# One feature map moved four and six steps sooner, its DMA transpose seven steps sooner and one matrix product one step later, in a fused attention and mixer kernel

## The chip, the cores and the metric

The kernel runs on one core of one Trainium2 chip. The metric is the device time in microseconds of one execution; smaller is better. All executions told of here ran at a granted TensorE clock of 0.99 to 1.00.

## The reference

Eight batches go through a linear attention and then through an MLP mixer. `phi` is the feature map elu(x) + 1.

```python
q_p, k_p = phi(q), phi(k)
kv = einsum('bhsd,bhse->bhde', k_p, v)
num = einsum('bhsd,bhde->bhse', q_p, kv)
den = einsum('bhsd,bhd->bhs', q_p, k_p.sum(axis=2))[..., None] + 1e-06
x = (num / den)                                   # to [batch, seq, 512]
h = maximum(x.transpose(0, 2, 1) @ w_tok1, 0) @ w_tok2
u = x + h.transpose(0, 2, 1)                      # token mixing
out = u + maximum(u @ w_ch1, 0) @ w_ch2           # channel mixing
```

## The kernel before

The program is one hand-ordered stream. The channel mixing of the batch pair that is ready is the "big" work of TensorE: `mm3` is the product with `w_ch1` (tile c_ps, line L480), `mm3_tail` the same for the rows left over (L494), `mm4` the product with `w_ch2` (h_ps, L506). A list `fill` names the step of this big work after which each small piece of the next batches' attention and token mixing is placed. The part that matters is the stage in which batches 0 and 1 finish, batch 2 is mixed and batch 3 is prepared.

```python
def phi(nm, n, c):                       # half c of batch n: exp on ScalarE, add and min on VectorE
    phi_exp(nm, n, 2 * c, 2); phi_add(nm, n, 2 * c, 2); phi_end(nm, n, 2 * c, 2)

def qtr_dma(n):                          # two DMA transposes, issued on SyncE: qp -> qT
    for a in range(2):
        nc.sync.dma_start_transpose(out=qT[n % 2][...], in_=qp[half[a]]...)   # ... cut

def utr_dma(n, rs):                      # u -> uT, half of the rows each
    nc.sync.dma_start_transpose(out=uT[b][...], in_=u[b][...])                # ... cut

def mm1(n): ...    # first mixing product, tile a_ps (L246); ScalarE writes relu to ar (L249)
def mm2(n, rs): ...# second mixing product, tile h_ps (L259); VectorE adds x and writes u (L271)
def nd_mm(n, c, rs): ...   # numerator and denominator, tile nd_ps (L208); qT is the weights

def mm4_end(p, t):                       # VectorE writes o_sb; every second tile two stores of 256 KB
    ...
    put = nc.sync if last else nc.gpsimd     # here: GpSimd
    (nc.scalar if last and e else put).dma_start(out=outv[...], in_=live["o"][half[e], 0:m])   # ... cut

def run(bigs, fill):
    for i, big in enumerate(bigs):
        big()
        for s, fn in fill:
            if s == i: fn()

# the stage in question: 3 + 9 steps of mm3, 3 of mm3_tail, 15 of mm4 (tiles 4 to 8)
at1 = {"kv": 8, "nd00": 10, ..., "nd21": 15,
       "mm1": 17, "mm2a": 18, "mm2b": 19, "mm2t": 21, "uta": 18, "utb": 19}
fill += [(at1[nm], fn) for nm, fn in steps(2)]
fill += [(s, lambda g=g: phi("q", 3, g)) for g, s in ((0, 19), (1, 22))]
fill += [(23, lambda: qtr_dma(3)), (23, lambda: load_all(4, "qkv"))]
fill += [(s, lambda g=g: prep_k(3, g)) for g, s in ((0, 24), (1, 26))]
run(big, sorted(fill, key=lambda e: e[0]))
# the next stage starts with mm3(2), which reads uT of batch 2; after its step 3 comes nd of batch 3, which reads qT
```

## Time and profile before

| | kernel before |
|---|---|
| time, median of 3 runs | 264.59 us (264.04 to 264.92) |
| span in the profile | 263.6 us |
| TensorE busy | 252.5 us, 96% |
| its one full stop after the start-up | 2.6 us, at 89.7 to 92.3 us |

A row of the timeline or of the chain is read as start in us, length in us, engine, line, operation, tiles (output, then inputs), count; what stands in square brackets is how long the engine had been idle and what ended that. Rows of the same operation are merged, so a row's length includes pauses between its instructions. The important rows are shown by the prediction below. One more view puts the stop into proportion: the busy time of each engine in two stretches of the kernel before (start and end, length, then busy time and instructions of TensorE, its weight loads, VectorE, ScalarE, GpSimd, then clock, DMA share and GB/s):

```profile
68.00:85.00 17.00, 16.91 (x83) 7.64 (x81) 11.60 (x20) 7.99 (x9) 1.53 (x3) 1.00 0.45 64
85.00:93.00 8.00, 5.42 (x97) 2.72 (x96) 1.70 (x5) 3.14 (x6) 1.93 (x4) 1.00 1.09 231
```

TensorE is full in the first stretch and lacks 2.58 us in the second, while the packet records fill the time of the 16 DMA engines (a share of 1.09; it is over 1 because records overlap, up to 28 at once in this stretch).

### The profile page before, as it was taken

The page shows a single profiled execution, that of the slowest core. Times are in us where ns is not written, and L with a number is a line of the kernel's source. Part 1 is how long each engine was busy: PE and PEld are TensorE (multiplying, and loading weights), DVE is VectorE, ACT ScalarE, POOL GpSimd, SP SyncE. Part 2 cuts the span into 40 slices and gives each one's busy share as a digit, 9 for nine tenths or more (in the row PEclk, how much of TensorE's full clock was granted, in tenths as well). Part 3 has the DMA queues.
Part 4 walks back from the last instruction along what each step waited for, and adds up shares of the span by engine and source line. Part 5 has one row for each costly group of instructions (what it writes and reads, how often), then busy time and mean ns, then how long its engine had stood idle before and what let it go on. Part 6 is the DMA issues. An engine that isn't in the chain of part 4 may idle for free.

```text
span 263.6 us, 5060 instructions
## 1 busy us (share of the span) xinstructions
PE 252.5 (96%) x2070; PEld 131.5 (50%) x2070; DVE 146.3 (56%) x283; ACT 130.8 (50%) x205; POOL 35.4 (13%) x58
## 2 busy tenths in 40 slices
PE   7789999999999699999999999999999999999994
PEld 3574465646644254445554554455564554444642
DVE  5865769866659185848564285838564272520122
ACT  5756763387292448425871368425870363027300
POOL 9660210110003100030001300030001300000000
PEclk9999999999999999999999999999999999999999
DMA  7999999999129992699998980761085500940043
GB/s 252 248 204 271 382 205 397 233 254 409 41 40 139 223 405 104 137 230 360 410 335 205 344 320 1 160 150 42 0 111 140 123 0 0 152 109 0 2 99 100
DMA packets 50087, 48.34 MB, mean 183 GB/s; under 512 B 30288, under 2 KB 35536, under 8 KB 50064
## 3 DMA queue, kind: packets, MB, share of 16 engines
q1 hardware_dynamic: 41904, 35.53, 46.0%
q0 software_dynamic: 7440, 11.44, 21.3%
q10 hardware_dynamic: 720, 1.05, 1.2%
q8 instruction: 16, 0.26, 0.4%
q14 instruction: 7, 0.06, 0.1%
HBM read 35.85 MB, written 9.44 MB: 172 GB/s over the span
## 4 chain that ended last, share of the span: by engine, by line
PE 80%; DMA 11%; ACT 3%; POOL 3%; issue 0%; SPq 0%; DVE 0%; ACTq 0%; POOLq 0%
PE h_ps L506 33%; PE c_ps L480 26%; PE a_ps L246 6%; PE c_ps L494 4%; DMA k_raw<-in_k_dram 4%; PE h_ps L259 4%; DMA wc<-in_moe_w_ch_dram 4%; DMA qT<-qp 3%; PE nd_ps L208 3%; PE kv_ps L167 2%; ACT e L124 1%; PE h_ps L543 1%; POOL qT L587 1%; ACT cr L487 1%; POOL cr L116 1%; PE h_ps L280 1%
## 5 line engine op out<-in xcount | busy, mean ns | idle before, releaser
L480 PE MATMUL c_ps<-uT,wc 128*128 128x512 bf16 x384 | 91.5, 379 | 0.0
L487 ACT ACTIVATE cr<-c_ps 128x512 bf16<-128x512 f32 x91 | 53.2, 599 | 77.1 <-PE c_ps L480 77.1
L506 PE MATMUL h_ps<-wc,cr 128*128 128x512 bf16 x372 | 85.1, 379 | 0.2
L506 PEld LDWEIGHTS <-cr 128*128 128x128 bf16 x372 | 35.7, 98 | 41.9 <-issue 1.6
L480 PEld LDWEIGHTS <-wc 128*128 128x128 bf16 x384 | 35.8, 98 | 36.7 <-issue 1.3
L528 POOL DMA_DIRECT2D out_dram<-o_sb x24 | 14.5, 606 | 153.2 <-DVE o_sb L523 152.9
L523 DVE TENSOR_TENSOR o_sb<-h_ps,u 128x512 f32<-128x512 f32 x31 | 21.2, 689 | 23.6 <-PE h_ps L506 23.4
L220 DVE TENSOR_TENSOR x<-nd_ps,den 128x512 bf16<-128x512 f32 (+1 forms) x42 | 25.3, 602 | 1.4
L124 ACT ACTIVATE e<-q_raw 128x1152 bf16<-128x1152 f32 x16 | 18.5, 1163 | 6.3 <-DMA q_raw<-in_q_dram 6.1
L271 DVE TENSOR_TENSOR u<-h_ps,x 128x1024 bf16<-128x1024 f32 x12 | 14.7, 1222 | 11.2 <-PE h_ps L259 11.2
L124 ACT ACTIVATE e<-k_raw 128x1152 bf16<-128x1152 f32 x16 | 18.7, 1168 | 4.2 <-DMA k_raw<-in_k_dram 4.2
L138 DVE TENSOR_TENSOR qp<-e,y 128x1152 bf16<-128x1152 bf16 x16 | 12.1, 759 | 13.6 <-ACT e L124 13.1
L217 DVE TENSOR_SCALAR den<-nd_ps 128x8 f32<-128x8 f32 (+1 forms) x42 | 6.8, 163 | 22.1 <-PE nd_ps L208 21.4
L208 PE MATMUL nd_ps<-kvbd,qT 128*128 128x130 bf16 x140 | 15.3, 223 | 2.6 <-DMA qT<-qp 2.6
L208 PEld LDWEIGHTS <-qT 128*128 128x128 bf16 x140 | 11.3, 98 | 12.0 <-DMA qT<-qp 2.9
L138 DVE TENSOR_TENSOR kp<-e,y 128x1152 bf16<-128x1152 bf16 x16 | 12.1, 756 | 8.0 <-ACT e L124 7.4
L246 PE MATMUL a_ps<-x,w 128*128 128x512 bf16 x56 | 14.4, 379 | 0.0
L149 ACT CAST vs<-v_raw 128x1152 bf16<-128x1152 f32 x12 | 13.9, 1159 | 0.0
L130 DVE TENSOR_SCALAR y<-k_raw 128x1152 bf16<-128x1152 f32 x16 | 12.0, 753 | 2.8 <-DMA k_raw<-in_k_dram 2.7
L533 DVE TENSOR_TENSOR o_sb<-h_ps,ut 128x512 f32<-128x512 f32 x4 | 2.8, 689 | 18.7 <-PE h_ps L506 18.7
L249 ACT ACTIVATE ar<-a_ps 128x512 bf16<-128x512 f32 x14 | 7.6, 594 | 10.9 <-PE a_ps L246 10.9
L259 PE MATMUL h_ps<-ar,w2p 128*128 128x512 bf16 x48 | 12.5, 379 | 0.1
(102 smaller groups left out, 207.9 us busy)
## 6 DMA issues: line engine op xcount, KB each, us to landing
k_raw<-in_k_dram SPq DMA_DIRECT2D x16, 576.0 KB, 9.0
q_raw<-in_q_dram SPq DMA_DIRECT2D x16, 576.0 KB, 7.7
v_raw<-in_v_dram SPq DMA_DIRECT2D x14, 576.0 KB, 11.0
out_dram<-o_sb POOLq DMA_DIRECT2D x24, 256.0 KB, 4.4
wc<-in_moe_w_ch_dram POOLq DMA_DIRECT2D x8, 384.0 KB, 10.3
out_dram<-o_sb SPq DMA_DIRECT2D x9, 128.0 KB, 2.3
out_dram<-o_sb ACTq DMA_DIRECT2D x7, 128.0 KB, 2.6
out_dram<-o_sb POOLq DMA_DIRECT2D x6, 128.0 KB, 5.9
```

The lines of the kernel that those rows point to most:

```text
L124: nc.scalar.activation(out=e, in_=f, func=AF.Exp)
L138: nc.vector.tensor_tensor(out=dst.transpose([0, 2, 1, 3]), in0=e.rearrange("p (i t d) -> p i t d", i=nj, t=T), in1=y.rearrange("p (i t d) ...
L208: nc.tensor.matmul(out=o[:, a], lhsT=qT[b][:, t0:t0 + 128], rhs=kvbd[b][:, c, a], start=True, stop=True)
L220: nc.vector.tensor_tensor(out=x[b][:, rs[0]:rs[0] + m, HG * D * g:HG * D * (g + 1)].rearrange("p r (h d) -> p r h d", h=HG), in0=v_[:, :, ...
L246: nc.tensor.matmul(out=ps[:, mt], lhsT=w1t[:, b, ms] if r == R else w1[:, r, ms], rhs=x[b][:, r, :], start=(r == 0), stop=(r == R))
L259: nc.tensor.matmul(out=ps[:, i], lhsT=w2v(kt, r, b), rhs=ar[b][:, kt, :], start=(kt == 0), stop=(kt == NT - 1 and not add))
L271: nc.vector.tensor_tensor(out=u[b][:, rs[0]:rs[0] + m], in0=ps[:, 0:m], in1=x[b][:, rs[0]:rs[0] + m], op=ALU.add)
L480: nc.tensor.matmul(out=ps, lhsT=wc1[:, kj, 128 * mc:128 * mc + 128], rhs=uT[b][:, :, kj], start=(kj == 0), stop=(kj == NDM - 1))
L487: nc.scalar.activation(out=cr[b][:, mc, :], in_=ps, func=AF.Relu)
L506: nc.tensor.matmul(out=ps, lhsT=crt[:, kc, :] if t == 8 else cr[b][:, kc, 128 * r:128 * r + 128], rhs=wc2[:, kc, :], start=(kc == 0), stop ...
L523: nc.vector.tensor_tensor(out=o, in0=ps, in1=u[b][:, r, :], op=ALU.add)
L528: (nc.scalar if last and e else put).dma_start(out=outv[2 * p + b, :, 2 * r0 + e:2 * r0 + e + 2 * m - 1:2], in_=live["o"][half[e], 0:m])
```

## The change

The intent: batch 3's q features exist earlier, so that their transpose is done long before its reader; and the second mixing product of batch 2 no longer follows so close behind the first that it waits for ScalarE's relu. The whole diff:

```diff
     at1 = {"kv": 8, "nd00": 10, "nd01": 11, "nd10": 12, "nd11": 13, "nd20": 14, "nd21": 15,
-           "mm1": 17, "mm2a": 18, "mm2b": 19, "mm2t": 21, "uta": 18, "utb": 19}
+           "mm1": 17, "mm2a": 19, "mm2b": 20, "mm2t": 21, "uta": 19, "utb": 20}
     fill = [(s, lambda g=g: phi("k", 2, g)) for g, s in ((0, 0), (1, 2))]
     fill += [(4, lambda: vcast(2, 0)), (5, lambda: vcast(2, 1, nc.vector.tensor_copy))]
     fill += [(at1[nm], fn) for nm, fn in steps(2)]
-    fill += [(s, lambda g=g: phi("q", 3, g)) for g, s in ((0, 19), (1, 22))]
-    fill += [(23, lambda: qtr_dma(3)), (23, lambda: load_all(4, "qkv"))]
+    fill += [(s, lambda g=g: phi("q", 3, g)) for g, s in ((0, 15), (1, 16))]
+    fill += [(16, lambda: qtr_dma(3)), (23, lambda: load_all(4, "qkv"))]
```

## The prediction

> **What bounds the kernel now.** I read the first part of the page, then the chain of waits in order of time, then who waited for whom, then the timeline around the one stretch that does not fit.
>
> ```profile
> PE 252.5 (96%) x2070; PEld 131.5 (50%) x2070; DVE 146.3 (56%) x283; ACT 130.8 (50%) x205; POOL 35.4 (13%) x58
> ```
>
> TensorE is busy 96% of the 263.6 us, everything else about half. So only TensorE's own idle time can be won, and other engines matter where they make it wait. The chain of the middle of the run is matmuls end to end except here:
>
> ```profile
> 70.86 2.17 PE a_ps L246 x10
> ...
> 73.56 0.60 ACT ar L249
> 74.20 0.81 PE h_ps L259 x3
> ...
> 76.73 6.87 PE h_ps L506 x32
> 83.60 8.62 DMA qT<-qp
> 92.27 0.35 PE nd_ps L208 x3
> ```
>
> The columns are start, length, what. Two things hang on something other than TensorE: at 73.56 to 74.20 ScalarE's relu eviction (ar) between the first mixing product of batch 2 (a_ps) and its second (h_ps L259), and at 83.60 to 92.27 a DMA transpose that brings batch 3's q features (qp) into the layout qT that the numerator/denominator product (nd_ps) loads as weights. The view of waits for TensorE alone, from 52 us to the end, has one line, so after the start-up this is the only full stop there is:
>
> ```profile
> PE nd_ps L208 <- DMA qT<-qp: 2.6, 1, 2.6
> ```
>
> The timeline shows how it came about (start, length, engine, line, how many):
>
> ```profile
> 73.06 1.08 ACT L249 ACTIVATE ar<-a_ps 128x512 bf16<-128x512 f32 x2 [4.39 <-PE a_ps L246]
> 73.72 1.28 PE L259 MATMUL h_ps<-ar,w2p 128*128 128x512 bf16 x4
> 76.29 2.96 SPq L464 DMA_TRANSPOSE uT<-u  x2
> 80.41 1.20 POOL L528 DMA_DIRECT2D out_dram<-o_sb  x2 [24.81 <-DVE o_sb L523]
> 80.88 0.76 DVE L138 TENSOR_TENSOR qp<-e,y 128x1152 bf16<-128x1152 bf16 x1
> 81.70 4.42 SPq L197 DMA_TRANSPOSE qT<-qp  x2
> 84.66 1.20 POOL L528 DMA_DIRECT2D out_dram<-o_sb  x2 [3.06 <-DVE o_sb L523]
> 85.20 1.89 PE L480 MATMUL c_ps<-uT,wc 128*128 128x512 bf16 x8
> 92.27 0.35 PE L208 MATMUL nd_ps<-kvbd,qT 128*128 128x130 bf16 x3 [2.58 <-DMA qT<-qp]
> ```
>
> The transposes are issued at 81.70, the moment the last qp is written (80.88 + 0.76), and then land slowly:
>
> ```profile
> DMA to landing us min/median/max: 5.5/7.1/8.6
> ```
>
> That line is for the two transposes of this stretch; over all twelve the same view gives 3.6/3.8/8.6. Two pairs of output stores (issued at 80.41 and 84.66, 256 KB each store) share the 16 DMA engines with them. Counting packets by size in the trace: from 82 to 84 us, 81 store packets of 4096 B and only 13 transpose packets of 256 B started; where transposes run alone (107 to 113 us) some 630 to 780 of them start per us. The 0.25 us at 73.72 is the other loss: four matmuls took 1.28 where the same four took 1.03 at 75.70, because the second half of ar ends only at 74.14.
>
> [...] the loads issued on SyncE from 86.22 on start to move (2304 B packets) only at 90 us, when the transpose before them is through. [...] Here about 700 packets of 256 B per us is some 180 GB/s[...], while 2304 B loads run at about 400 GB/s (94 to 96 us). The measured rate is used below. [...] Here the matmuls of the stages stand end to end at their steady 0.86 us per four, so the 96% does mean that the engine's stream is full.
>
> **The change, part by part.** No instruction is added or removed; comparing the order of instructions, TensorE takes four L506 matmuls ahead of the two groups of h_ps L259, VectorE and ScalarE move the q feature map ahead, SyncE issues qT before uT.
>
> *Feature map of q(3) to steps 15 and 16, transposes to 16.* ScalarE stands idle 4.39 us before 73.06, so the two exponentials (2.22 us for both) fit in 68.7 to 70.9 at no cost; their input landed at 61.2. VectorE's last x of batch 2 ends at 70.01; two adds and two mins (0.75 and 0.76 each, 3.1 us together) then run to about 73.1. It was idle 3.45 us before 75.04, so the next needed output (u) is not delayed, only the store staging of output tile 4, whose PSUM bank is not wanted until 82.6. The transposes then issue at about 73.2 and 74.6, with no other DMA in flight (last load landed at 68.1). At the 3.8 us median they land at 77.0 and 78.4, ten us ahead of the need at 89.7. **Gain: 2.58 us**, all of it on the path, because TensorE has no other wait later to absorb it.
>
> *Second mixing product one step later.* Between a_ps and h_ps now stand eight L506 matmuls (1.73 us) instead of four (0.86): a_ps ends at 73.02, so h_ps starts at 74.75, after ar is done at 74.14. **Gain: 0.25 us.** It delays u: the halves end on TensorE at 75.6 and 77.3 instead of 75.0 and 76.7, so u is written by about 76.9 and 78.7, and the two uT transposes issue at about 76.9 and 78.8 instead of 76.29 and 78.02.
>
> *What this collides with.* Before, the second uT landed 4.33 us after issue, at 82.35; its reader (c_ps at 85.20) had 2.85 us to spare. With 0.25 us won, the reader now comes at 84.95. A landing as fast as before would be at about 83.1: 1.8 us to spare. But the first pair of stores, which in the kernel before was held back to 80.41 by the q feature map on VectorE, now leaves at about 77.6 and 78.2: in front of the second uT, and the second pair comes at about 83.3. That is the position in which the first qT stood before (stores 1.29 and 0.70 us ahead of it): it needed 5.49 us. 78.8 + 5.5 = 84.3, still 0.65 us in time. By packets: about 128 store packets at 0.4 us each over 16 engines are 3.2 us, 78.7 to 81.9, in which transposes hardly move; some 1,600 of uT's 2,048 packets are then left, 2.4 us at 670 per us, to 84.3, and 0.7 us to the semaphore: 85.0. So the reader waits between nothing and about 1 us, and some 2.5 us if the second pair of stores also gets in front. I put the mean at **0.4 us** (half the chance on none, three in ten on up to 1 us, two in ten on more; the last are partly bounded because the stores must first be written).
>
> *Sum.* 264.59 - 2.58 - 0.25 + 0.4 = 262.2; as no wait is the likeliest single case (261.8), I say 262.1.
>
> **Rivals.**
> 1. *uT takes qT's place as the late transfer.* For it: the working above, under 1 us of slack by either estimate. [...] At worst, a landing 8.6 us after issue (as the second qT did) is 87.4, a wait of 2.45 us, which leaves 264.59 - 2.83 + 2.45 = 264.2: no visible gain.
> 2. *The transfer was hidden anyway, or another input is late at the same place.* nd_ps also needs kvbd, but ScalarE wrote that by 88.62, and one nd_ps matmul ran at 89.47, before the stop. I give this little weight. It would leave at least 263.5.
> 3. *VectorE or ScalarE becomes the bound around 70 us.* If the feature map got in front of ar or of batch 2's last x, mm1 would wait up to 2 us: 264. The order on each engine shows it behind x and in a 4.39 us hole of ScalarE, so I nearly rule it out.
> 4. *Later stages give it back.* From 92 us on, all loads, transposes and stores shift with the matmuls; uT has 4.7 us to spare at 115.37 (landed 110.62) and 7.2 at 147.24 (landed 140.07). Batch 4's loads even leave earlier, at about 80 instead of 86.22. I see nothing to give back.
>
> **Range and chances.** Full gain is 261.8; runs of one kernel spread by about 0.4 us to each side, so the low end is 261.3. A wait for uT of some 1.5 us plus spread gives 263.7 at the high end. Two per cent is 5.3 us, twice all the idle time there is to win, and the worst rival ends at parity: the chance of within 2% is 0.98, with 0.01 to each side.
>
> **What would show it.** Right: the wait of nd_ps for qT is gone from TensorE's waits, the qT transposes issue at about 73 and land within 4 us, h_ps L259 takes 1.03 per four without a pause after ar, SyncE's uT issues near 77 and 79. For rival 1 look for a new wait of c_ps L480 or its weights for uT at about 85 us; its length is what is lost. Wrong for me would be: a uT wait over 1.5 us, a pause before a_ps at 70.9, or a new stop past 95 us.

## The result, and the profile after

| | before | after |
|---|---|---|
| time, median of 6 runs | 264.61 us (263.84 to 264.92) | 262.45 us (262.01 to 262.63) |
| ratio, with 95% interval | | 0.9922 (0.9906 to 0.9938) |
| span in the profile | 263.6 us | 260.4 us |
| TensorE waits of the view from 52 us on | one, 2.6 us | none |

A ratio is the mean time of one kernel's fast runs over the mean of the other's of the same rounds, so it is not quite the ratio of the medians. Executions over 1.5% slower than the fastest of the same kernel are left out of the means. The change saves 2.2 us of the median: real, but within 2%.

The chain of waits after, at the places that answer to those of before (start, length, what):

```profile
72.89 1.73 PE h_ps L506 x8
74.62 0.86 PE h_ps L259 x4
...
84.98 1.73 PE c_ps L480 x8
86.70 0.71 PE kv_ps L167 x70
87.41 1.83 PE c_ps L480 x8
89.25 0.23 PE nd_ps L208 x4
```

The step over ScalarE and the DMA transpose are out of the chain: every row is TensorE, each starting where the row before it ends. The timeline of the kernel after:

```profile
72.93 1.09 ACT L249 ACTIVATE ar<-a_ps 128x512 bf16<-128x512 f32 x2 [2.28 <-PE a_ps L246]
72.99 2.75 SPq L197 DMA_TRANSPOSE qT<-qp  x2
74.45 1.03 PE L259 MATMUL h_ps<-ar,w2p 128*128 128x512 bf16 x4
76.77 3.75 SPq L464 DMA_TRANSPOSE uT<-u  x2
77.64 1.20 POOL L528 DMA_DIRECT2D out_dram<-o_sb  x2 [22.18 <-DVE o_sb L523]
84.81 1.89 PE L480 MATMUL c_ps<-uT,wc 128*128 128x512 bf16 x8
89.08 0.40 PE L208 MATMUL nd_ps<-kvbd,qT 128*128 128x130 bf16 x4
```

The transposes of q are issued at 73.0, not 81.7; h_ps takes 1.03 us for its four, not 1.28; and nd_ps runs its four at 89.08 without a stop. The stores leave at 77.6, between the two transposes of u. Time from issue to landing of the two q transposes, and then of the two u transposes, in the kernel after (least, median, most):

```profile
DMA to landing us min/median/max: 3.4/3.6/3.7
DMA to landing us min/median/max: 3.1/4.4/5.7
```

So q is no longer slowed, and u is: its second half, issued at 78.50, landed at 84.22, 0.6 us before its reader at 84.81. The two stretches of the table above, in the kernel after:

```profile
68.00:85.00 17.00, 16.89 (x80) 7.76 (x80) 12.26 (x21) 7.93 (x9) 2.40 (x4) 1.00 0.58 131
85.00:93.00 8.00, 8.00 (x118) 4.37 (x117) 3.95 (x11) 4.75 (x9) 1.07 (x2) 1.00 1.01 356
```

The second stretch is full. (A few matmul records are missing from the trace after; counts of matmuls are not compared.)

**An accounting that does not close yet.** The two profiles differ by 3.1 us of span, the medians by 2.16 us. From the first mixing product (70.86 before, 70.73 after) to the end of the first nd_ps group (92.62 and 89.48) the profiles differ by 21.76 - 18.75 = 3.01 us. Of that, 0.26 lies ahead of c_ps (the pause after ar), and 2.75 between c_ps and the end of the group: the stop of 2.58 and 0.17 for starting the matmuls again (0.22 + 0.35 against 0.40 us for the group). So the profile of before showed a gain larger than the timed runs had. The experiments had to explain that too.

### The profile page after: what moved, and what is told of

Its sections match the earlier page's. It is cut to its first block, busy times and chain, and to the rows that moved or that the text cites. A ratio compares the mean times of both kernels' runs of the same rounds, so it can differ in the third digit from the quotient of the medians.

```text
span 260.4 us, 5043 instructions
## 1 busy us (share of the span) xinstructions
PE 251.7 (97%) x2052; PEld 131.7 (51%) x2070; DVE 146.3 (56%) x283; ACT 130.8 (50%) x205; POOL 35.4 (14%) x58
## 4 chain that ended last, share of the span: by engine, by line
PE 88%; POOL 4%; DMA 3%; ACT 3%; DVE 1%; issue 1%; POOLq 0%
PE h_ps L506 33%; PE c_ps L480 32%; PE a_ps L246 5%; PE c_ps L494 4%; PE h_ps L259 4%; PE nd_ps L208 3%; DMA w<-in_moe_w_tok_dram 3%; PE kv_ps L167 2%; POOL w2p L451 1%; PE h_ps L543 1%; ACT e L124 1%; POOL qT L587 1%; POOL cr L116 1%; PE h_ps L280 1%; ACT cr L487 1%
## 5 line engine op out<-in xcount | busy, mean ns | idle before, releaser
L130 DVE TENSOR_SCALAR y<-q_raw 128x1152 bf16<-128x1152 f32 x16 | 12.2, 765 | 0.0
```

The lines of the kernel that those rows point to most:

```text
L130: nc.vector.tensor_scalar(out=y, in0=f, scalar1=1.0, scalar2=1.0, op0=ALU.add, op1=ALU.max)
```

## The experiments

**Theories.** (A) The stop exists because store packets get in front of the q transposes on the DMA engines. It is then a race, whose length differs from run to run. (B) The stop has a fixed length of 2.6 us and the transposes were simply issued too late; the 0.7 us between the sum of the prediction (2.83 us) and the 2.16 us measured are then a new wait for uT, in timed runs but not in the profile. And: do the two parts of the change add up, as the prediction has it?

Eleven runs were made. Eight are in the table; b1 to b3, the kernel before profiled again, follow it.

| run | what | median us (range), 6 runs | before in the same rounds | ratio (95%) |
|---|---|---|---|---|
| c0_after | the change, again | 262.25 (262.09 to 262.62) | 263.79 (262.39 to 264.75) | 0.9946 (0.9919 to 0.9973) |
| e1_q_only | only the q part | 262.45 (262.26 to 263.06) | as above | 0.9952 (0.9927 to 0.9978) |
| e6_after_stores_held | the change, first stores held | 262.2 (261.91 to 262.5) | as above | 0.994 (0.9915 to 0.9965) |
| e4_before_stores_held | before, all four stores held | 262.21 (261.98 to 262.92) | as above | 0.9943 (0.9918 to 0.9969) |
| e2_mm2_only | only the mixing product | 262.5 (262.29 to 262.76) | 264.44 (263.72 to 265.59) | 0.9926 (0.9908 to 0.9944) |
| e3_map_only | the change, transposes late | 263.52 (263.33 to 264.3) | as above | 0.9969 (0.9947 to 0.999) |
| e5_mm2_later | the change, product yet later | 262.23 (261.82 to 262.5) | as above | 0.9915 (0.9896 to 0.9933) |
| e7_pair2_held | before, second stores held | 262.59 (262.22 to 262.89) | 264.29 (262.59 to 266.45), 10 fast runs | 0.9939 (0.99 to 0.9979) |

All gave correct results. One thing shows at once: the 11 runs of the kernel before spread over 2.4 and 1.9 us in the first two lots (6 runs over 1.1 us in the first comparison), the 6 runs of every version without the stop over 0.5 to 0.9 us. (In the third lot the kernel before has, beside the slow run, one of 266.45 us at a clock of 0.994, counted as fast; without these two its spread is 2.0 us. That run also flatters the ratio of e7.)

### The kernel before, profiled three more times

No edit.

> The kernel before again, for another profile. Theory (the stop for qT is a race between transpose and store packets, and so differs from run to run, which is why the timed runs of this kernel spread from 262.4 to 264.9 us): a wait between 0 and 2.6 us, and the run's time is about 262.4 us plus this wait. Rival (the stop is always 2.6 us, and the spread is from elsewhere): a wait of 2.5 to 2.7 us whatever the run's time.

> The kernel before once more, for its profile. Theory (the stop is a race and differs): wait plus 262.4 us gives this run's time within 0.5 us; the wait is anything from 0 to 2.6 us. Rival: 2.5 to 2.7 us again.

> The kernel before once more, for its profile. Theory and rival as for the one just before: the wait differs between 0 and 2.6 us and accounts for the run's time over 262.4 us, or it is 2.5 to 2.7 us whatever the time.

The line of TensorE's waits from 52 us on, in the runs b1, b2 and b3, in this order:

```profile
PE nd_ps L208 <- DMA qT<-qp: 1.9, 1, 1.9
```

```profile
PE nd_ps L208 <- DMA qT<-qp: 1.2, 1, 1.2
```

```profile
PE nd_ps L208 <- DMA qT<-qp: 1.2, 1, 1.2
```

| profile of before | wait us | time of that run us | time less wait |
|---|---|---|---|
| the first | 2.58 | 265.34 | 262.76 |
| b1 | 1.86 | 264.31 | 262.45 |
| b2 | 1.19 | 263.81 | 262.62 |
| b3 | 1.18 | 263.94 | 262.76 |

(b1 to b3 are single runs, of unknown state; their clock was 0.998 to 1.0.) The wait is not fixed, and what is left after taking it away is the same within 0.3 us. The profile that the prediction was made from had the longest stop of the four, and its run, 265.34 us, was slower than all three timed runs that the prediction quotes. That closes the accounting: the timed runs' stop is on the mean shorter than 2.6 us. The last column has a mean of 262.65 us, so the median of 264.61 us holds, by estimate, a stop of 1.96 us; the 0.20 us that are left of the 2.16 us fit the shorter pause after ar. The fastest runs of the kernel before, 262.39 and 262.59 us, leave no room for more than a few tenths of a stop; none of those was profiled, so that they had none is an inference.

### Stores held, in the kernel before and in the kernel after

The edit keeps the stores of some output tiles back until a given transpose has landed (a dependency of the store on that transfer). It is shortened here:

```diff
-                    (nc.scalar if last and e else put).dma_start(out=outv[...], in_=live["o"][half[e], 0:m])
+                    # as a closure that is called later, with a dependency on the gate
+                    after(put.dma_start(out=outv[...], in_=o[half[e], 0:m]), gate)
+    # e4: fill += [(23, lambda: release(5, "qT_dma")), (27, lambda: release(7, "qT_dma"))]
+    # e7: fill += [(27, lambda: release(7, "qT_dma"))]
+    # e6: fill += [(20, lambda: release(5, "uT_dma"))]
```

e4 holds both pairs in the kernel before, where nothing else is moved.

> The kernel before with nothing moved, except that the stores of output tiles 4 to 7 of the first pair of batches wait until the second qT transpose has landed. Theory (the transposes were late because store packets held them up): qT lands within 4 us of issue, near 85.6 and 87, before the need at 89.5; the stop of 2.6 us is gone; the pause of 0.25 us after ar stays; time 0.25 us over the changed kernel, about 262.7 us. Rival (issue at 81.7 is simply too late, or something else slows the transposes): qT still lands after 89.5, time over 263.7 us.

Issue to landing of its two q transposes, and what its stores waited for:

```profile
DMA to landing us min/median/max: 3.5/3.7/3.8
```

```profile
87.17 2.39 POOL L535 DMA_DIRECT2D out_dram<-o_sb  x4 [31.84 <-DMA qT<-qp]
```

The transposes were issued at 81.4 and 82.8, as late as before, and landed at 85.0 and 86.6, well ahead of nd_ps at 89.2. There is no TensorE wait, and the time is that of the changed kernel. The stores alone made the transposes late (3.5 and 3.8 us from issue to landing here, 5.2 to 8.6 us in the four profiles of the kernel before); the late issue did not. The pause after ar is still there (1.28 us for the four matmuls of h_ps), yet the median is not 0.25 us over c0 as expected; differences of 0.2 us are within what these medians can tell.

e7 holds only the second pair.

> The kernel before with only the second pair of stores (output tiles 6 and 7) held until the second qT transpose has landed; the first pair goes as before. In the kernel before, 63 packets of one of these stores ran between the two qT transposes. Theory[...]: qT a is late as before, landing 5.5 us after issue near 87; qT b follows it at once and lands near 88.5 to 89.0, just before the need at 89.2 to 89.5; no wait or under 0.3 us; 262.3 to 262.8 us. Rival (the first pair alone makes qT too late): qT b lands after 90.5, a wait over 1 us, over 263.4 us.

Issue to landing of its two q transposes:

```profile
DMA to landing us min/median/max: 4.9/5.3/5.8
```

The first, behind the first pair of stores, took 5.8 us, as in the kernel before (5.2 to 5.8 in its four profiles). The second took 4.9 us instead of 7.2 to 8.6, landed at 88.5, and nd_ps did not stop. Packets started per microsecond show what went with it (store packets are 4096 B, transpose packets 256 B; counted from the traces):

```text
            kernel before              e7: second pair held
from us   stores  transposes         stores  transposes
 82          46        0                48        0
 83          35       13                39       19
 84          25      132                23      207
 85           5      479                 2      537
 86          37      536                 0      890
 87          26      214                 0      650
 88           1      540                 0        1
 89          15      354                 0        0
```

In the kernel before, most of one 256 KB store (63 packets at 86 and 87 us) runs between the two transposes, and the pair's second store runs among the last 86 packets of the second transpose (from 89.75 us on). Holding the pair takes away both, and the stop with them; which of the two stores costs more was not tested. The picture also differs from profile to profile: at 86 and 87 us the four profiles of the kernel before start 63, 22, 32 and 36 store packets, at 88 and 89 us 16, 105, 89 and 99. In all four the second transpose lands within 0.4 us of the pair's second store (92.22 and 92.06 us in the first).

The columns also show uneven counts, though less than the first rows suggest. Where no store is about (after, c0, e1, e4, e5, e6), the first packet of the first q transpose starts 1.18 or 1.19 us after its issue. With that delay after the issue at 81.70, no transpose packet was to be expected here before 82.88 us; from 82.88 to 84 us the kernel before started 43 store packets and 13 transpose packets.

e6 holds the first pair in the changed kernel, to see whether its timed runs hide a wait for uT.

> The changed kernel with the first pair of stores of this stage held until the second uT transpose has landed. Both: uT b lands within 4.3 us of its issue instead of 5.7. Theory: no change of time, within 0.15 us of the changed kernel, as uT was in time. Rival (hidden uT wait in the timed runs): 0.3 to 0.7 us faster than the changed kernel.

Issue to landing of its two u transposes:

```profile
DMA to landing us min/median/max: 3.1/3.6/4.1
```

uT's second half landed 4.1 us after its issue instead of 5.7 (at 82.3), and the median went from 262.25 to 262.2 us. Nearly two microseconds of slack more bought nothing, so the changed kernel does not wait for uT to a degree that these medians can show. Theory B's hidden wait, expected to be worth 0.3 to 0.7 us here, is not seen.

### Each part alone

e1 has only the q part:

```diff
-           "mm1": 17, "mm2a": 19, "mm2b": 20, ..., "uta": 19, "utb": 20}      # of the kernel after
+           "mm1": 17, "mm2a": 18, "mm2b": 19, ..., "uta": 18, "utb": 19}
```

> The q feature map and its transposes early, the second mixing product at its old steps. Theory (the stop for qT is all gone, uT is in time in the changed kernel's timed runs too): loses the 0.25 us pause after ar again, so 0.25 us over the changed kernel, about 262.7 us; uT b lands near 82.5 to 83.5. Rival (the 0.7 us missing from the sum of 2.83 us are a wait for uT that the timed runs have and the profile does not show): this kernel has uT 0.6 us earlier, so it is as fast as the changed kernel or up to 0.4 us faster, 262.0 to 262.4 us.

262.45 us against 262.25 of c0 in the same rounds: 0.20 us slower. In its profile h_ps takes 1.28 us again and there is no wait:

```profile
73.51 1.28 PE L259 MATMUL h_ps<-ar,w2p 128*128 128x512 bf16 x4
```

The size fits the 0.25 us, but the ranges overlap, so by time alone it is not settled; the profile shows the pause.

e2 has only the second mixing product one step later:

```diff
-           "mm1": 17, "mm2a": 18, "mm2b": 19, ..., "uta": 18, "utb": 19}      # of the kernel before
+           "mm1": 17, "mm2a": 19, "mm2b": 20, ..., "uta": 19, "utb": 20}
```

> The kernel before with only the second mixing product one step later. Theory (u is later, and VectorE then writes the second half of u behind the q feature map, so uT b and qT are both issued later and behind the stores): uT b issues near 80.4 and lands near 85 to 86, qT b lands near 91 to 93; TensorE waits for uT up to 1.2 us and for qT up to 2.5 us; the 0.25 us of ar are lost in these waits; 264.0 to 265.5 us, at or over the kernel before. Rival (the parts add: this one is worth its 0.25 us alone): 0.25 us under the kernel before of the same rounds, no uT wait.

Both expectations were wrong. It runs in 262.5 us, 1.9 us under the kernel before: nearly everything that the whole change gives. The timeline of its DMA issues and its first nd_ps group:

```profile
77.08 4.54 SPq L464 DMA_TRANSPOSE uT<-u  x2
81.89 3.64 SPq L197 DMA_TRANSPOSE qT<-qp  x2
```

```profile
79.46 1.62 POOL L528 DMA_DIRECT2D out_dram<-o_sb  x2 [23.68 <-DVE o_sb L523]
84.86 1.20 POOL L528 DMA_DIRECT2D out_dram<-o_sb  x2 [3.77 <-DVE o_sb L523]
```

```profile
89.64 0.40 PE L208 MATMUL nd_ps<-kvbd,qT 128*128 128x130 bf16 x4
```

The VectorE order came out as expected (uT b issued at 80.33, q at 81.89 and 84.25, all later than before). What the expectation had wrong was the order in which the packets started. By the packet counts, store 1 ran first (80 to 82 us), then uT b, then store 2 with q following, then the second q transpose right behind the first one (86 to 87.5 us), with store 3 starting at 87.15, when it was nearly through. The same bytes as in the kernel before, but no store between the two q transposes. They landed at 86.3 and 89.1, the second 0.5 us ahead of nd_ps; uT b landed at 85.24, 0.14 us ahead of c_ps at 85.38. So this version has the time of the changed kernel by a hair's breadth. Why store 3 goes between the transposes in one version and behind them in the other was not settled: in the kernel before SyncE was busy with issuing the second q transpose until 86.1 and store 3 was issued by 85.3; in e2 the same two ends are 85.53 and 85.46, which alone would not decide it.

### The map early, the transposes late; and the product later still

e3 is the changed kernel with the transposes put back behind those of u:

```diff
-    fill += [(16, lambda: qtr_dma(3)), (23, lambda: load_all(4, "qkv"))]
+    fill += [(23, lambda: qtr_dma(3)), (23, lambda: load_all(4, "qkv"))]
```

> The changed kernel with the feature map early but the two qT transposes issued after those of uT, as before. Theory (early issue matters only because it puts the transposes in front of the stores): uT as before or a little faster, qT a issues near 80.5 right behind uT b, with one pair of stores ahead and one at 83.4; qT b lands at 87 to 91, need at 89.1; a wait of 0 to 2 us that differs from run to run; median 262.3 to 264 us, spread over 1 us. Rival (getting the feature map off VectorE before the second mixing product is what won, the place of the transposes does not matter): as fast as the changed kernel, 262.0 to 262.6 us, with no wait and no spread.

```profile
PE nd_ps L208 <- DMA qT<-qp: 0.9, 1, 0.9
```

This is its one wait of TensorE from 52 us on. The median is 263.52 us, 1.3 us over e5, the version without the stop in the same rounds. Having the feature map off VectorE is not what wins; on the contrary, e3 differs from e2 only in the early map and is 1.0 us slower. Its trace suggests why: the stores then leave at 77.9 and 83.7 instead of 79.5 and 84.9, and the packets of the third store run between the two q transposes again (64 of them at 85 and 86 us). That this order costs the 1.0 us was not tested by itself.

e5 moves the second mixing product of the changed kernel one step later still:

```diff
-           "mm1": 17, "mm2a": 19, "mm2b": 20, "mm2t": 21, "uta": 19, "utb": 20}
+           "mm1": 17, "mm2a": 20, "mm2b": 21, "mm2t": 22, "uta": 20, "utb": 21}
```

> The changed kernel with the second mixing product yet one step later (0.86 us). It measures the slack of uT. Theory (0.4 to 0.6 us of slack in the changed kernel, uT b behind the stores): both uT transposes now stand behind the first pair of stores; uT b lands at 85 to 87.5, TensorE waits 0.3 to 2.8 us for it at 84.8; 262.7 to 265 us with a larger spread. Rival (the stores delay uT by a bounded amount and it keeps landing near 84.5): no wait, 262.0 to 262.6 us.

The rival was right: 262.23 us, no wait. uT b was issued 1.2 us later than in the changed kernel (79.68 against 78.50) and landed at 84.15, just as there (84.22). That would fit stores ahead of it that set when it goes. But the first pair of stores left 0.8 us earlier too (76.83 against 77.64), and uT a now landed at 83.30 instead of 79.85, so the run does not separate the two. No version beat the changed kernel by more than these medians can tell. The changed kernel has the pause gone and the q transposes 11 us early (landed 78.06, needed 89.08), as e5 and e6 have; for uT it has only tenths (0.6 us, in c0 84.37 against 84.74). e6 has 2.2 us there (82.30 against 84.54) at the same time, e1 2.4 us (82.59 against 84.99) with the pause back.

## Why the prediction was right or wrong

The time, 262.45 us, lies in the range and 0.35 us over the point value. By its steps:

- **Bound and place of the loss: right.** TensorE's stop for qT was the only one, and its removal came through to the end: from the end of the first nd_ps group to the end of the span the two profiles need the same, 170.95 us each.
- **The q part on the timeline: right.** Expected issue 73.2 and 74.6, landing 77.0 and 78.4; measured 72.99 and 74.38, 76.43 and 78.06. It fitted into the holes of ScalarE and VectorE.
- **"Gain: 2.58 us" for the stop: mis-sized.** The step took the stop of one profile for that of every run. Four profiles have 2.58, 1.86, 1.19 and 1.18 us. Against the runs of the first comparison both parts together gave 2.16 us; run again in other rounds (c0) 1.5 us, and e5, which has both and the product one step later still, 2.2 us. Within that one profile the term was even a little short, by the 0.17 us for the restart.
- **"Gain: 0.25 us" for the pause after ar: the profile shows it** (1.28 to 1.03 us); in the times it is no more than a hint (e1, 0.20 us).
- **The 0.4 us mean wait for uT: zero.** uT b landed at 84.22, right at the early end of the two workings (84.3 and 85.0), before the reader, and e6 and e5 show no such wait. This term and the one for the stop were both off and partly cancelled, which is luck in the number: 2.83 - 0.4 = 2.43 against 2.16 measured. The later of the two workings put most of uT's 2,048 packets behind the first stores; measured, uT a had landed at 79.85, and only the 1,024 of uT b stood behind them. Its other figures were near what the trace of before shows: 0.4 us for a store packet (the 81 that started from 82 to 84 us took 0.37 us on the mean) and 0.7 us from the last packet to the landing (0.48 and 0.62 us for the two u transposes).
- **The sum as a sum of parts: wrong.** The prediction gave the stop to the q part alone and 0.25 us to the mixing product. Each part alone removes the stop (e1: 262.45, e2: 262.5 us), and so does holding the stores (e4, e7). What the q part adds over e2 is safety, not time: 11 us of slack for qT in place of 0.5.
- **The reading of 81 store packets and only 13 transpose packets from 82 to 84 us: too strong.** 38 of the 81 store packets started before a transpose packet was to be expected (82.88 us, see e7); after that it was 43 against 13. That stores made the transposes late stands on e4, not on this count.
- **Rival 1 was named rightly and did not happen.** uT did become the late transfer and took 5.7 us, close to the 5.5 of the analogy. Rivals 2 to 4 did not show.

## What to carry to other kernels

Before sizing a gain from one profile, compare its run's time with the timed runs. Here a stop that ended with a DMA among stores was 1.2 to 2.6 us long from profile to profile, and the wide spread of the old kernel's times was its sign (1.1 to 2.4 us, against 0.5 to 0.9 us for the versions without the stop). When a transfer that something waits for is slow, look at which other transfers stand in front of it: holding those back (e4, 262.21 us), or a changed order of arrival that nobody planned (e2, 262.5 us), was worth as much here as issuing it earlier (e1, 262.45 us). Where times are equal, compare the slack of every transfer: e2 holds by tenths of a microsecond for qT (0.5 us), the changed kernel by tenths for uT (0.6 us).

## What the traces show of the transposes and stores, and what they leave open

- A 256 KB store has 64 packet records. From 82.88 to 84 us the kernel before started 43 store and 13 transpose packets, and 63 or 64 store packets ran between two q transposes (first profile, e3). What decides the order of the packets was not settled.
- The two q transposes of the changed kernel, alone, started 2,304 packets of 256 B from 74.2 to 77.5 us: about 700 per us, some 180 GB/s (in single slices of 1 us of the kernel before up to 1,074, 275 GB/s). Loads in packets of 2304 B moved some 400 GB/s (94 to 96 us of the kernel before). These transposes are of 262 or 295 KB each; larger ones were not run.
- A q transpose of this stage took 3.4 to 3.9 us from issue to landing without stores, 4.4 to 8.6 us with two or three stores of 256 KB about.
